# Two loads of a two-layer decode kernel, each issued as two pieces of uneven row counts

## The chip, the cores and the metric

The kernel runs on one core of one Trainium2 chip. The metric is the device time of one execution in microseconds.

## What is computed

Two layers, each an attention over a window of a cached K and V followed by a gated MLP, are applied twice in turn with the same weights to four vectors of 640 numbers, all in f32. Cut to what matters, the reference is:

```python
W = 1024                                   # the last quarter of 4096 positions
x = x + A(layernorm(x))                    # attention: 32 heads of 128, one query each
x = x + M(layernorm(x))                    # MLP: 640 -> 1728 -> 640
x = x + A(layernorm(x))
x = x + M(layernorm(x))
# A: q = x @ wq; p = softmax(q k^T / sqrt(128)) over the window; (p v) @ wo
# M: gate = x @ W_gate; h = gate * (gate > 0) * (x @ W_up); h @ W_down
```

Each number of K, V and the weights is used for only four vectors.

## The kernel before

Nearly all the work is bringing in data. The host lays K, V and the weights out as three long arrays with 128 rows, one per partition: `heads` (K, V, wq and wo of 27 heads, read in both layers), `kept` (the same of the last five heads, in the groups K0 and K1, read once and kept in the core's memory for layer two), and `mlp` (the MLP's weights). One buffer, `store`, of 128 partitions by 51,840 columns, takes all of it. A plan written at the start (`put`, `stretch`) lists which columns of which array go to which columns of `store`, in order. `load` (from L202) takes the plan's next piece whenever its place in `store` is free and issues one DMA from SP for it (L211); `done` and `free` mark columns as used up and call `load` again. SP's order is the plan's order, and the DMA queue is first in, first out on each of the 16 DMA engines. Before it reuses one of its eight landing counters, SP also waits until the load that had that counter last has landed.

Layer one (`attention(0)`) goes through nine groups of heads, K0 and K1 last. For a group TensorE computes scores (L396), VectorE and ScalarE the softmax (L403, L407), TensorE transposes the probabilities (L411) and multiplies by V (L427), then projects with wo (L461). At the end of the attention the last V product is copied out by VectorE and ScalarE (L432, L433), `free(*BACK)` gives columns back to the plan, the last projections follow, then the norm (`normalized`, L314 to L336) and the MLP (`forward`): gate and up (L519), the nonlinearity (L528, L529), a transpose (L536, L541) and W_down (L550, L561) into `y`. Layer two repeats this, with K0 and K1 first. The result is copied from `y` (L586) and stored (L587).

Two pieces of the plan matter here. The last of kept V, with the last 1,024 columns of the array up to `FRONT`, holds the last two of eight chunks of V of the last head of K1; in the plan kept W_o and wq come after it, then the first MLP weights. The last piece of all is a W_down block of 640 columns up to `MLP`, used by the last four products at L550 in layer two. Both come as 128 rows in one DMA.

Of the kernel before, what the change touches and what calls it, by code (L numbers as in the profile page):

```python
# [13 lines left out]
P = 128  # L14
# [39 lines left out]
MLP = WD1 + 3 * WD  # L54
# [7 lines left out]
FRONT = KEPT * 2 * (D + KV)  # L62
# [36 lines left out]
def decode_kernel(ctx: ExitStack, tc: tile.TileContext, x, source, sel, out):  # L99
    nc = tc.nc  # L100
# [10 lines left out]
    store = big.tile([P, STORE], F32, name="store")  # L111
# [8 lines left out]
    def put(layer, row, to, *cuts):  # L120

        for lo, hi in zip(cuts, cuts[1:]):
            assert hi - lo <= MOST and to % 64 == 0 and lo in known[row] and hi in known[row], (row, lo, hi)
            assert to + hi - lo <= STORE, (row, lo, hi, to)
            plan.append((layer, row, lo, hi, to))
            to += hi - lo
        return to

    def stretch(layer, lo, end, to):

        while lo < end:
            hi = near(min(end, lo + MOST))
            if to + hi - lo > LAP:
                to = 0
            to = put(layer, "heads", to, lo, hi)
            lo = hi
        return to
# [4 lines left out]
    def near(c, row="heads"):  # L142

        return max(x for x in ROWS[row][2] if x <= c)
# [10 lines left out]
    to = stretch(0, HELD, turn, FIRST)  # L155
# [8 lines left out]
    lo = put(0, "mlp", STORE - D, 0, D) - STORE + D  # L164
# [9 lines left out]
    to = put(1, "heads", FRONT, k, k + 1536, k + 2560, k + 3584)  # L174
# [3 lines left out]
    lo = k + 4096  # L178
    to = put(1, "heads", AHEAD[1], lo, lo + 1024, lo + 2048, lo + 3072, lo + 5120, lo + 8704)
    assert to == HOME  # L180
    lo, to = lo + 8704, HOME + BACK[1] - BACK[0]
    for n in 4608, 6144, 9728:
        hi = near(lo + n)
        to = put(1, "heads", to, lo, hi)
        lo = hi
    hi = near(lo + 4608)
    to = put(1, "heads", to, lo, hi)
    lo, hi = hi, near(hi + STORE - to)
    put(1, "heads", to, lo, hi)
    last = near(heads_end - 24704)  # L190
    to = stretch(1, hi, last, 0)
    for lo, hi in (last, near(last + 12480)), (near(last + 12480), heads_end):
        to = put(1, "heads", to if to + hi - lo <= STORE else 0, lo, hi)
    cuts = [0, 7040, 12160, GU0 + 3 * GU, WD1 + WD, MLP - 4 * D, MLP - 2 * D, MLP - D, MLP]
    for lo, hi in zip(cuts, cuts[1:]):
        to = put(1, "mlp", to if to + hi - lo <= STORE else 0, lo, hi)

    plan.reverse()

    live = [False] * STORE  # L200
# [2 lines left out]
    def load():  # L203

        if not held:
            nc.sync.dma_start(out=first_q, in_=source["heads"][:, :HELD])
        while plan and not any(live[plan[-1][4]:plan[-1][4] + plan[-1][3] - plan[-1][2]]):
            layer, row, lo, hi, to = plan.pop()
            live[to:to + hi - lo] = [True] * (hi - lo)
            held.setdefault((layer, row), []).append((lo, hi - lo, to))  # L210
            nc.sync.dma_start(out=store[:, to:to + hi - lo], in_=source[row][:, lo:hi])  # L211

    def free(a, b):
        live[a:b] = [False] * (b - a)
        load()
# [16 lines left out]
    def done(layer, row, lo, n):  # L232

        if row == "kept" and layer == 0:
            return
        if row == "kept":
            for p in range(lo, lo + n):
                if BACK[0] <= p < BACK[1]:
                    live[HOME + p - BACK[0]] = False
                elif not (AHEAD[0] <= p < AHEAD[1] or HOME <= p < HOME + BACK[1] - BACK[0]):  # L240
                    live[p] = False
        else:
            for first, m, p in held[key(layer, row)]:
                a, b = max(lo, first) - first, min(lo + n, first + m) - first
                if a < b:
                    live[p + a:p + b] = [False] * (b - a)
        load()
# [9 lines left out]

    probs = work.tile([P, W], F32, name="probs")
    load()
    gates = work.tile([P, 512], F32, name="gates")  # L260
    sel_sb = const.tile([P, P + 32], F32, name="sel_sb")
# [384 lines left out]
```

## Time and profile before

| | us |
|---|---|
| median of 3 runs (732.97 to 734.17) | 733.54 |
| the profiled execution | 733.02 |
| its span, first to last instruction | 731.2 |
| TensorE busy | 440.8 |
| VectorE busy | 76.1 |
| ScalarE busy | 50.5 |

The span is what the page's shares refer to; 1.8 us of the profiled execution lie around it. The lists further down name instructions by line, engine and operation, with the tiles written and read; what stands in brackets is the idle time of the engine before the instruction, and what ended it. The DMA share of a window is the mean busy share of the 16 DMA engines. In the list of queues, the columns are packets, megabytes, and the time of the packets as a share of 16 engines' span; q1 is SP's queue, q10 ScalarE's, and `instruction` queues bring in the program itself.

### The profile page before, as it was taken

To read this page: it belongs to the slowest core of one execution; us is meant where nothing else is said; L and a number is where in the kernel's file an instruction comes from. 1 tells how busy PE (TensorE), PEld (TensorE's weight loads), DVE (VectorE), ACT (ScalarE), POOL (GpSimd) and SP (SyncE) were. 2 spreads that over 40 slices of the span, in tenths; PEclk is the share of its full clock that TensorE was granted. 3 is DMA by queue.
4 is the path that set the end of the run, shared out by engine and by line. 5 is a ranking of instruction groups with operands and counts; after the bars stand their busy time and mean duration, and the time that the engine had idled before them with its cause. 6 is when DMAs were issued, how large, how long until landed. Compare 5 with 4: busy or idle time off the path is not lost.

```text
span 731.2 us, 8241 instructions
## 1 busy us (share of the span) xinstructions
PE 440.8 (60%) x3755; PEld 140.9 (19%) x3755; DVE 76.1 (10%) x280; ACT 50.5 (7%) x93; POOL 0.2 (0%) x4
## 2 busy tenths in 40 slices
PE   0846565655555555519778995465656556555576
PEld 0211111111111111103333231021111012111233
DVE  1111000010010101002101221001011010101011
ACT  0200000000000000000301210000000000000100
POOL 0000000000000000000000000000000000000000
PEclk9978787877777787759999999677778677877999
DMA  9999999999999999999999999999999999999996
GB/s 414 400 445 438 445 438 405 439 444 438 422 430 438 422 443 442 422 428 421 421 401 410 437 426 452 427 445 425 442 438 411 445 440 444 410 435 432 428 425 286
DMA packets 13290, 311.80 MB, mean 426 GB/s; under 512 B 1476, under 2 KB 1732, under 8 KB 6984
## 3 DMA queue, kind: packets, MB, share of 16 engines
q1 hardware_dynamic: 13104, 311.19, 99.1%
q8 instruction: 29, 0.48, 0.2%
q10 hardware_dynamic: 152, 0.09, 0.0%
q14 instruction: 5, 0.04, 0.0%
HBM read 311.19 MB, written 0.08 MB: 426 GB/s over the span
## 4 chain that ended last, share of the span: by engine, by line
DMA 75%; PE 23%; DVE 1%; issue 1%; ACT 0%; SPq 0%; ACTq 0%; DVEq 0%
DMA store<-in_heads 56%; PE ps L396 9%; DMA store<-in_kept 9%; DMA store<-in_mlp 7%; PE po L427 5%; DMA sel_sb<-in_sel 3%; PE qp L364 1%; PE pp L411 1%; PE y L461 1%; PE qp L371 1%; PE pp L396 1%; PE pp L519 1%; PE qt L383 1%; PE ot L451 0%; PE y L550 0%
## 5 line engine op out<-in xcount | busy, mean ns | idle before, releaser
L396 PE MATMUL ps<-store,qT 128*4 128x512 f32 x976 | 154.1, 711 | 119.9 <-DMA store<-in_heads 97.9
L427 PE MATMUL po<-store,pT 128*16 128x512 f32 (+1 forms) x1028 | 151.9, 708 | 122.4 <-DMA store<-in_heads 116.5
L427 PEld LDWEIGHTS po<-store,pT 128*16 128x16 f32 x1028 | 32.5, 109 | 226.9 <-issue 118.5
L396 PEld LDWEIGHTS ps<-store,qT 128*4 128x4 f32 x976 | 28.4, 95 | 227.3 <-DMA store<-in_heads 110.0
L403 DVE TENSOR_REDUCE nm<-ps 128x1 f32<-128x1024 f32 x17 | 20.8, 1225 | 255.4 <-PE ps L396 255.4
L407 ACT ACTIVATE probs<-ps,nm 128x1024 f32<-128x1024 f32 x17 | 18.9, 1113 | 328.8 <-DVE nm L403 328.8
L421 DVE COPY pT<-pp 128x16 f32<-128x16 f32 x128 | 17.1, 169 | 135.1 <-PE po L427 135.1
L461 PE MATMUL y<-store,oT 128*4 128x160 f32 x512 | 23.6, 317 | 10.6 <-DMA store<-in_heads 9.0
L438 ACT COPY gates<-po 128x512 f32<-128x512 f32 x16 | 9.4, 586 | 247.6 <-PE po L427 247.6
L519 PE MATMUL pp<-store,xT 128*32 128x256 f32 (+1 forms) x300 | 21.8, 363 | 6.7 <-DVE gates L529 3.1
L411 PE MATMUL pp<-sel_sb,probs 128*128 128x128 f32 x144 | 20.8, 293 | 0.0
L411 PEld LDWEIGHTS pp<-sel_sb,probs 128*128 128x128 f32 x144 | 18.7, 155 | 0.0
L364 PE MATMUL qp<-store,xT 128*32 128x512 f32 (+2 forms) x124 | 18.5, 586 | 0.0
L444 DVE RECIPROCAL r<-so 128x16 f32<-128x16 f32 x18 | 4.6, 257 | 131.2 <-PE so L442 131.2
L461 PEld LDWEIGHTS y<-store,oT 128*4 128x4 f32 x512 | 12.8, 90 | 19.6 <-DMA store<-in_heads 9.4
L371 PE MATMUL qp<-store,xT 128*32 128x512 f32 (+3 forms) x38 | 15.1, 505 | 0.0
L376 DVE TENSOR_SCALAR gates<-qp,rstd 128x512 f32<-128x512 f32 (+2 forms) x18 | 12.4, 690 | 17.5 <-PE qp L371 16.0
L291 PE MATMUL y<-probs,sel_sb 4*4 4x160 f32 x8 | 0.7, 444 | 21.2 <-DMA sel_sb<-in_sel 21.2
L519 PEld LDWEIGHTS pp<-store,xT 128*32 128x32 f32 x300 | 10.0, 109 | 16.3 <-DMA store<-in_mlp 7.1
L550 PE MATMUL y<-store,hT 128*4 128x160 f32 x208 | 10.3, 299 | 3.5 <-DMA store<-in_mlp 3.4
L383 PE MATMUL qt<-sel_sb,gates 128*128 128x128 f32 x64 | 12.3, 315 | 0.0
L451 PE MATMUL ot<-sel_sb,gates 128*128 128x128 f32 x72 | 11.3, 277 | 1.2 <-DVE gates L432 1.2
(79 smaller groups left out, 133.2 us busy)
## 6 DMA issues: line engine op xcount, KB each, us to landing
store<-in_heads SPq DMA_DIRECT2D x20, 7936.0 KB, 45.2
store<-in_heads SPq DMA_DIRECT2D x3, 8128.0 KB, 36.0
store<-in_mlp SPq DMA_DIRECT2D x15, 640.0 KB, 6.6
store<-in_kept SPq DMA_DIRECT2D x2, 4096.0 KB, 40.7
store<-in_heads SPq DMA_DIRECT2D x1, 8000.0 KB, 43.7
store<-in_heads SPq DMA_DIRECT2D x1, 7744.0 KB, 46.0
store<-in_heads SPq DMA_DIRECT2D x1, 7552.0 KB, 35.8
store<-in_heads SPq DMA_DIRECT2D x1, 7424.0 KB, 34.6
```

The costliest lines, as they stand in the source:

```text
L364: nc.tensor.matmul(qp[g][32 * c:32 * c + 32, a:b], xT[:, B * c:B * c + 32], part(layer, "q", g, c * n + a, b - a), start=True, stop=c > 0 ...
L371: nc.tensor.matmul(qp[g][32 * a:32 * a + 32, a * m:a * m + m], xT[:, B * c:B * c + 32], part(layer, "q", g, c * n + a * m, m), start=False ...
L376: nc.vector.tensor_scalar(gates[:, :len(HEADS[g]) * P], qp.pop(g), rstd, SCALE, op0=ALU.mult, op1=ALU.mult)
L383: nc.tensor.transpose(qt[:, i], gates[:, i * P:(i + 1) * P], ident)
L396: nc.tensor.matmul(to[32 * b:32 * b + SIDE, j, :], qT[:, at:at + SIDE], part(layer, "k", h, lo, 512), start=i == 0, stop=i == n - 1, tile_ ...
L403: nc.vector.tensor_reduce(nm[g], to.rearrange("p j n -> p (j n)"), axis=AX.X, op=ALU.max, negate=True)
L407: nc.scalar.activation(probs, sc.pop(g).rearrange("p j n -> p (j n)"), AF.Exp, bias=nm.pop(g), accum_out=sums[g])
L411: nc.tensor.transpose(pp[:, c // 4, c % 4 * P:c % 4 * P + P], probs[:, c * P:(c + 1) * P], ident)
L421: nc.vector.tensor_copy(to[:, 4 * j:4 * j + 4], pp[:, j].rearrange("p (c x) -> p c x", c=4)[:, :, i:P:32])
L427: nc.tensor.matmul(po[32 * a:32 * a + SIDE * B, x:z], t[:, at:at + SIDE * B], part(layer, "v", h, c * 512 + x, z - x), start=i == 0 and c ...
L461: nc.tensor.matmul(y[32 * a:32 * a + B], o[:, i], part(layer, "o", h, a * QUARTER, QUARTER), start=False, stop=last and h == HEADS[g][-1], ...
L519: nc.tensor.matmul(gus[j][32 * g:32 * g + 32, :2 * n], xT[:, B * c:B * c + 32], get(layer, "mlp", lo, 2 * n), start=c == 0, stop=c == KC - ...
```

## The change

```diff
+    split = {(0, "kept", FRONT): 68, (1, "mlp", MLP): 92}
     plan.reverse()
 ...
             layer, row, lo, hi, to = plan.pop()
             live[to:to + hi - lo] = [True] * (hi - lo)
             held.setdefault((layer, row), []).append((lo, hi - lo, to))
-            nc.sync.dma_start(out=store[:, to:to + hi - lo], in_=source[row][:, lo:hi])
+            rows = split.get((layer, row, hi), P)
+            for p, z in (0, rows), (rows, P):
+                if p < z:
+                    nc.sync.dma_start(out=store[p:z, to:to + hi - lo], in_=source[row][p:z, lo:hi])
```

Two loads of the plan are issued as two DMAs each: the last V block of layer one's kept part as rows 0 to 67 and rows 68 to 127, and the last W_down block of layer two as rows 0 to 91 and rows 92 to 127. The bytes, their places and the order of all other loads stay. Lines after the change are four further down.

On SP, around the kept V block, before (a row is one DMA, with rows x columns and the counters that it waits for: DMAHW0 to DMAHW7 are the eight landing counters):

```order
L211 DMA store<-in_kept 128x3072 [waits PE_49]
L211 DMA store<-in_kept 128x1024 [waits PE_49]
L211 DMA store<-in_kept 128x1920
L211 DMA store<-in_kept 128x1280 [waits DMAHW4_49]
L211 DMA store<-in_mlp 128x640 [waits DMAHW5_49,PE_49]
L211 DMA store<-in_mlp 128x1280 [waits DMAHW6_49]
L211 DMA store<-in_mlp 128x1280 [waits DMAHW7_49]
L211 DMA store<-in_mlp 128x1280 [waits DMAHW0_49]
L211 DMA store<-in_mlp 128x1280 [waits DMAHW1_49,PE_49,Activation_49]
```

The same place after the change:

```order
L215 DMA store<-in_kept 128x3072 [waits PE_49]
L215 DMA store<-in_kept 68x1024 [waits PE_49]
L215 DMA store<-in_kept 60x1024
L215 DMA store<-in_kept 128x1920 [waits DMAHW4_49]
L215 DMA store<-in_kept 128x1280 [waits DMAHW5_49]
L215 DMA store<-in_mlp 128x640 [waits DMAHW6_49,PE_49]
L215 DMA store<-in_mlp 128x1280 [waits DMAHW7_49]
L215 DMA store<-in_mlp 128x1280 [waits DMAHW0_49]
L215 DMA store<-in_mlp 128x1280 [waits DMAHW1_49]
L215 DMA store<-in_mlp 128x1280 [waits DMAHW2_49,PE_49,Activation_49]
```

The piece of 60 rows takes the counter that the next load had, and every load from there on waits for a landing one further down the list.

On SP at the end of the program, before:

```order
L211 DMA store<-in_mlp 128x2560 [waits PE_49]
L211 DMA store<-in_mlp 128x1280 [waits PE_49]
L211 DMA store<-in_mlp 128x640 [waits PE_49]
L211 DMA store<-in_mlp 128x640 [waits DMAHW3_49,PE_49]
L587 DMA out_x<-probs 128x160 [waits DMAHW4_49,DVE_49,Activation_49]
```

And after:

```order
L215 DMA store<-in_mlp 128x2560 [waits PE_49]
L215 DMA store<-in_mlp 128x1280 [waits PE_49]
L215 DMA store<-in_mlp 128x640 [waits PE_49]
L215 DMA store<-in_mlp 92x640 [waits DMAHW4_49,PE_49]
L215 DMA store<-in_mlp 36x640 [waits DMAHW5_49]
L591 DMA out_x<-probs 128x160 [waits DMAHW6_49,DVE_49,Activation_49]
```

The last piece waits for one more landing before it is issued. On TensorE the order is the same; the first product that reads the split block at L427, and the one at L550, wait for two counters in place of one.

## The prediction

> **What bounds the kernel now.** I read the page first: the span, the DMA queues, and the chain that ended last.
>
> ```profile
> span 731.2 us, 8241 instructions
> q1 hardware_dynamic: 13104, 311.19, 99.1%
> q8 instruction: 29, 0.48, 0.2%
> q10 hardware_dynamic: 152, 0.09, 0.0%
> DMA 75%; PE 23%; DVE 1%; issue 1%; ACT 0%; SPq 0%; ACTq 0%; DVEq 0%
> ```
>
> The 16 DMA engines are busy 99.1% of the span with the loads that SP issues, and 75% of the chain is DMA. The kernel is one stream of 311 MB; compute matters only where it lets the queue run dry, or at the very end. So I read the end next, the timeline of the last microseconds and the windows of half a microsecond over the same stretch (in a window: length, busy times, clock, share of the 16 engines at work, GB/s).
>
> ```profile
> 726.92 0.11 PEld L550 LDWEIGHTS y<-store,hT 128*4 128x4 f32 x8 [0.29 <-DMA store<-in_mlp]
> 727.70 0.11 PEld L550 LDWEIGHTS y<-store,hT 128*4 128x4 f32 x8 [0.67 <-DMA store<-in_mlp]
> 727.70 0.46 PE L550 MATMUL y<-store,hT 128*4 128x160 f32 x8 [0.32 <-DMA store<-in_mlp]
> 728.22 0.32 DVE L586 COPY probs<-y 128x160 f32<-128x160 f32 x1 [4.12 <-PE y L550]
> ...
> 723.50:724.00 0.50, 0.39 (x5) 0.14 (x1) 0.07 (x1) 0.00 (x0) 0.00 (x0) 1.00 0.80 328
> 724.50:725.00 0.50, 0.35 (x12) 0.30 (x16) 0.00 (x0) 0.00 (x0) 0.00 (x0) 1.00 0.61 246
> 725.50:726.00 0.50, 0.42 (x14) 0.07 (x4) 0.00 (x0) 0.00 (x0) 0.00 (x0) 1.00 0.44 174
> 726.50:727.00 0.50, 0.50 (x20) 0.19 (x12) 0.00 (x0) 0.00 (x0) 0.00 (x0) 1.00 0.32 123
> 727.00:727.50 0.50, 0.38 (x8) 0.03 (x8) 0.00 (x0) 0.00 (x0) 0.00 (x0) 1.00 0.15 56
> ```
>
> TensorE waits for the last load until 727.70 and everything after it is fixed. But the engines do not end together: the share falls from 0.80 to 0.61, 0.44, 0.32 and 0.15, so the first are out of work at about 723.9, about seven of 16 work at 725.5, five until nearly 727, and the last lands just before 727.70: a spread of 3.8 us. Each load waits for its slowest engine. The 29 instruction packets, 0.48 MB on the same engines, are the plainest cause that the page offers: an engine that fetches falls behind and, in a full stream, stays there.
>
> While few engines work each keeps its pace: 123 GB/s over 0.32 of 16 is 24 GB/s, and in full streams (below) 415 over 16 is 25.9. So nothing that all 16 share sets the pace. It is either the engine itself, or the place in the memory that it writes, which before I take to be the same eight partitions in every load of 128 rows. No row separates the two, and the change hangs on that.
>
> **Which engines the pieces use.** The loads' counts tell how rows are dealt out.
>
> ```profile
> L211 SPq DMA_DIRECT2D store<-in_heads x45: 327/328/538, 1.2 to 658.0; - x45
> L211 SPq DMA_DIRECT2D store<-in_mlp x34: 327/328/785, 347.0 to 697.0; - x34
> L211 SPq DMA_DIRECT2D store<-in_kept x10: 327/328/432, 220.9 to 341.5; - x10
> ```
>
> With the first load and the store these are 91 transfers of 128 rows, and 13104 over 91 is 144: 128 rows and 16 closings, one an engine. ScalarE's queue, 152 packets, had one such transfer (144) and x with four rows: four rows and four closings, so four engines. The largest divisor up to 16 fits both; read so, 68 rows take four engines (17 each), 60 take 15 (4 each), 92 take four (23 each), 36 take twelve (3 each). The other end, an even deal over all 16 whatever the count, would make the change worth nothing.
>
> [...]
>
> **What a row costs.** A 2,560-byte row: the last two loads of 128x640 released TensorE at 726.92 and 727.70, 0.78 us for eight rows an engine, 0.098 us each. A 4,096-byte row: 25.9 GB/s from the row below, 0.158 us.
>
> ```profile
> 357.00:359.00 2.00, 0.26 (x8) 0.07 (x8) 0.00 (x0) 0.45 (x2) 0.00 (x0) 1.00 1.00 415
> 360.00:368.00 8.00, 6.43 (x114) 3.64 (x108) 1.65 (x6) 1.47 (x5) 0.00 (x0) 1.00 1.01 417
> 371.00:373.00 2.00, 1.97 (x20) 0.56 (x18) 0.00 (x0) 0.00 (x0) 0.00 (x0) 1.00 0.96 316
> 358.96 2.17 PE L427 MATMUL po<-store,pT 128*16 128x512 f32 x16 [1.74 <-DMA store<-in_kept]
> 360.09 0.12 PEld L427 LDWEIGHTS po<-store,pT 128*16 128x16 f32 x4 [0.16 <-DMA store<-in_kept]
> store<-in_kept SPq DMA_DIRECT2D x1, 512.0 KB, 19.5
> store<-in_mlp SPq DMA_DIRECT2D x4, 640.0 KB, 6.3
> store<-in_mlp SPq DMA_DIRECT2D x3, 256.0 KB, 5.8
> DMA to landing us min/median/max: 5.1/21.3/62.4
> ```
>
> **The change, part by part.**
>
> *Two more issues on SP, and every later wait on a landing moved one load down.* An issue takes 0.33 us of an SP that mostly waits. The split V block is issued 19.5 us before it lands and the last W_down block 30 us before (the chain below), so both pieces are queued in time. The order rows show that a later load waits for the landing of one further down, for instance the W loads behind the V block; they land 18.1 us after issue, so a load's landing later (about 5 us at most, SP's longest wait for kept loads) stays covered. I cost all of it at nothing; without that cover it would be those microseconds. TensorE's last V products (L427) and last W_down products (L550) now wait for two landings in place of one: behind the first stand the projection, the norm and the gates, behind the second only a copy and the store.
>
> ```profile
> store<-in_mlp SPq DMA_DIRECT2D x3, 640.0 KB, 18.1
> SPq L211 <- DMA store<-in_kept: 10.3, 3, 4.5
> 696.96 30.70 DMA store<-in_mlp
> ```
>
> *The V block.* Four engines get 17+4 = 21 rows in place of eight, 13 x 0.158 = 2.05 us more; eleven get four, 0.63 less; one gets none, 1.26 less. *The last W_down block.* Four get 26 in place of eight, 18 x 0.098 = 1.76 more; eight get three, 0.49 less; four none, 0.78 less.
>
> *If the place sets the pace* (my forecast): the four engines now write rows of other engines' partitions, while those write too, and each has half. The V block's 17 rows take up to 5.4 us, with the other four 6.0, against 1.26: 4.7 more. They start from a lead that I estimate at 2.5 us (3.8 at the end, with 11 of the 29 instruction packets behind it at 357), so the block lands 2.2 later; bounds 0 (lead 3.8, mild sharing) and 4.7 (no lead).
>
> ```profile
> q8 instruction: 11, 0.18, 0.2%
> ```
>
> TensorE reached that block 0.16 us before it landed, so the last V product, the projection, the norm and the first gate go later by as much, and with them the loads issued as buffers come free. There the stream is thin: these land 5.8 to 6.3 us after issue where 5.1 is the shortest of the run, and at 371 to 373 the rate is already 316 of 417 GB/s. About 1 us of lateness is covered, 1.2 becomes idle engines and stays to the end. At the end the early ones of the four start the block at about 723.1; 23 rows at half pace and three more take 4.8 us, to 727.9, and one that is 1.2 us later goes to 729.1 against 727.66: +0.2 to +1.4, I take +0.6. What the late engines are relieved of does not help here, since the same partitions still take the same bytes. Sum: 1.2 + 0.6 = +1.8 us.
>
> [...]
>
> **The rivals.**
>
> *The engine sets the pace* (faster). Then it matters only who is late. At the end the five that work until 727 cannot all be among the four that get nothing, so the latest is relieved by 0.49; the four must stay under that: if they are early they end by 725.5 + 1.76 = 727.26 at worst. Gain 0.45. At the V block the late eleven are 0.63 earlier; part of that is kept, since late engines are not those that idle at 371 to 373 (between 0 and 0.63; I take 0.4). Sum -0.85. For it: each engine's pace does not depend on how many work. Against it: it needs the four to be early ones too; the decision point is 3.8 - 1.76 = 2.0 us of lead.
>
> *The four are late ones* at their own pace: the end is 1.76 later and the V block 2.05 less 1 of cover: +2.8.
>
> *It does not do what it says*: the rows are dealt evenly, or gains and losses cancel: 0, give or take 0.3.
>
> *All four write the same partitions at a time* (rows dealt in turn): five share one place, 23 rows x 0.098 x 5 = 11 us, some +8.
>
> **How the numbers follow.** The profiled execution took 733.02 (span 731.2 and 1.8 around it); the median of the runs shown is 733.54, 0.52 more, and I put the forecast beside the median. Forecast: 733.02 + 1.8 = 734.8, so 735.3 (alone 734.2 to 737.0), chance 0.47: no row favours the place over the engine, but the first rival needs a second condition and this does not. Engine: 732.2, so 732.7, 0.32. Nothing: 733.5, 0.11. Four late: 736.3, 0.06. All in one place: 741.5, 0.04. The range, 732.2 to 737.4, leaves out the lower part of the engine case and the last one. A measurement of this kernel can tell about 0.2%, 1.5 us. Slower by more: most of the forecast (0.40) and the last two (0.10), 0.50. Within: the rest of the forecast, nearly all of the engine case and the third, 0.46. Faster by more: 0.04.
>
> **What would show it.** In the windows of the end the share stays flat and drops late if the four engines are last, and falls in steps that end before 727.6 if the engine case holds. In the timeline TensorE's wait for the last kept V load ends near 362 in place of 360.09 by the forecast, and at 360 by the rival. At 371 to 373 the rate falls below 316 by the forecast. The first place that breaks it: packets of both pieces at normal pace with TensorE's V product unmoved; then sharing does not exist.

## The result, and the profile after

The changed kernel took 738.33 us (median of 4 runs, 737.61 to 740.37) against 733.27 for the kernel before beside it (4 runs): a ratio of 1.0071 with a 95% interval of 1.0049 to 1.0094, 5.1 us slower. The profiled execution took 737.61 (before 733.02). The forecast was +1.8, with 737.4 as the upper end of the range.

The page of the changed kernel, span and SP's queue:

```profile
span 735.8 us, 8245 instructions
q1 hardware_dynamic: 13107, 311.19, 99.0%
```

The same bytes in three packets more. Two whole loads have 32 closings; four pieces on 4, 15, 4 and 12 engines have 35. So the closings are those of the dealing that the prediction read; the count gives their sum, not each piece's.

Next the windows about the V block, first of the changed kernel, then those rows of the kernel before that the prediction did not show. The last three columns are TensorE's clock, the share of the 16 DMA engines and GB/s.

```profile
355.00:361.00 6.00, 1.91 (x16) 0.42 (x16) 0.00 (x0) 1.96 (x3) 0.00 (x0) 1.00 1.04 273
357.00:359.00 2.00, 0.19 (x4) 0.00 (x0) 0.00 (x0) 0.00 (x0) 0.00 (x0) 1.00 1.02 239
359.00:361.00 2.00, 0.00 (x0) 0.00 (x0) 0.00 (x0) 0.00 (x0) 0.00 (x0) 1.00 1.04 224
361.00:363.00 2.00, 1.63 (x8) 0.36 (x11) 0.00 (x0) 0.00 (x0) 0.00 (x0) 0.58 0.95 301
363.00:365.00 2.00, 1.93 (x12) 0.22 (x6) 0.00 (x0) 0.00 (x0) 0.00 (x0) 0.56 0.99 411
371.00:373.00 2.00, 1.41 (x29) 1.03 (x23) 0.44 (x2) 0.57 (x2) 0.00 (x0) 1.00 0.94 362
373.00:376.00 3.00, 3.00 (x44) 1.27 (x36) 0.00 (x0) 0.09 (x1) 0.00 (x0) 1.00 1.00 348
385.00:410.00 25.00, 22.06 (x269) 8.76 (x271) 2.87 (x10) 4.12 (x9) 0.00 (x0) 1.00 1.02 399
```

```profile
355.00:361.00 6.00, 3.95 (x32) 0.93 (x32) 0.37 (x5) 2.45 (x4) 0.00 (x0) 1.00 0.99 414
361.00:363.00 2.00, 1.40 (x22) 0.83 (x24) 0.79 (x3) 0.75 (x2) 0.00 (x0) 1.00 1.03 420
385.00:410.00 25.00, 23.03 (x268) 9.45 (x268) 5.21 (x14) 5.33 (x11) 0.00 (x0) 1.00 1.03 416
```

Read the last two columns together. From 357 to 361 the share is 1.02 and 1.04, so all 16 engines have work all the time, and yet they move 239 and 224 GB/s. Not four engines but the whole stream goes at a little over half pace. From 355 to 363 that is (414 - 273) x 6 + (420 - 301) x 2 = 1,084 KB less than before, 2.6 us at 415 GB/s.

The traces also hold the time of every single packet, and a row of a load is one packet. The V block's 128 rows of 4,096 bytes took 159 ns each before; after the change half of them took 272 ns or more. So the pieces did not go at normal pace, the first sign by which the prediction would have been broken.

TensorE at the same place in the changed kernel, then the marker where layer two's first queries begin, after and before:

```profile
361.37 3.56 PE L431 MATMUL po<-store,pT 128*16 128x512 f32 x16 [4.18 <-DMA store<-in_kept]
362.99 0.23 PEld L431 LDWEIGHTS po<-store,pT 128*16 128x16 f32 x6 [0.64 <-DMA store<-in_kept]
365.07 0.42 DVE L436 COPY gates<-po 128x256 f32<-128x256 f32 x1 [10.19 <-PE po L431]
...
402.36 0.52 PE L368 MATMUL qp<-probs,xT 128*32 128x384 f32 x2
```

```profile
361.25 0.42 DVE L432 COPY gates<-po 128x256 f32<-128x256 f32 x1 [5.88 <-PE po L427]
...
398.31 0.52 PE L364 MATMUL qp<-probs,xT 128*32 128x384 f32 x2
```

(Lines behind the edit moved down by four.) The wait for the load *ahead* of the V block, which the change does not touch, ends at 361.37 in place of 358.96; the V block's own at 362.99 in place of 360.09; the copy behind the V products comes 3.8 later, layer two's queries 4.05 later. The end of the changed kernel:

```profile
727.00:728.00 1.00, 0.79 (x17) 0.29 (x9) 0.17 (x1) 0.00 (x0) 0.00 (x0) 1.00 0.74 279
728.00:729.00 1.00, 0.07 (x4) 0.07 (x8) 0.00 (x0) 0.00 (x0) 0.00 (x0) 1.00 0.83 260
729.00:730.00 1.00, 1.00 (x32) 0.68 (x32) 0.00 (x0) 0.00 (x0) 0.00 (x0) 1.00 0.69 187
730.00:731.00 1.00, 0.20 (x8) 0.00 (x0) 0.00 (x0) 0.00 (x0) 0.00 (x0) 1.00 0.42 133
732.92 0.33 DVE L590 COPY probs<-y 128x160 f32<-128x160 f32 x1 [4.92 <-PE y L554]
```

The last copy comes at 732.92 in place of 728.22, 4.70 later: 4.05 were there at layer two's start, so 0.65 was added behind it. The stream is some 4 us later here, and from 728 to 730 the share is 0.83 and 0.69 where 4 us earlier it was 0.61 and 0.44 before; then it drops. That is nearer to the forecast's sign (flat, and late) than to the rival's. The engines still at work are slower, too: 260 GB/s over 0.83 of 16 is 20 GB/s each, 187 over 0.69 is 17, where before 246 over 0.61 was 25 and 174 over 0.44 was 25.

### The profile page after: what moved, and what is told of

Same layout as the page of the kernel before. It is cut to its first block, busy times and chain, and to the rows that moved or that the text cites. A ratio compares the mean times of both kernels' runs of the same rounds, so it can differ in the third digit from the quotient of the medians.

```text
span 735.8 us, 8245 instructions
## 1 busy us (share of the span) xinstructions
PE 440.5 (60%) x3755; PEld 140.5 (19%) x3755; DVE 76.0 (10%) x280; ACT 50.5 (7%) x93; POOL 0.2 (0%) x4
## 4 chain that ended last, share of the span: by engine, by line
DMA 73%; PE 23%; another core or an unknown queue 1%; DVE 1%; issue 1%; ACT 0%; SPq 0%; ACTq 0%; DVEq 0%
DMA store<-in_heads 53%; PE ps L400 10%; DMA store<-in_kept 9%; DMA store<-in_mlp 8%; PE po L431 6%; DMA sel_sb<-in_sel 3%; PE qp L368 1%; PE y L465 1%; PE pp L415 1%; PE qp L375 1%; PE pp L400 1%; PE pp L523 1%; PE qt L387 1%; PE ot L455 0%
## 5 line engine op out<-in xcount | busy, mean ns | idle before, releaser
L431 PE MATMUL po<-store,pT 128*16 128x512 f32 (+1 forms) x1028 | 155.1, 722 | 127.6 <-DMA store<-in_heads 118.7
L400 PE MATMUL ps<-store,qT 128*4 128x512 f32 x976 | 150.9, 698 | 118.3 <-DMA store<-in_heads 95.8
```

Of the source, the lines that this page charges most:

```text
L400: nc.tensor.matmul(to[32 * b:32 * b + SIDE, j, :], qT[:, at:at + SIDE], part(layer, "k", h, lo, 512), start=i == 0, stop=i == n - 1, tile_ ...
L431: nc.tensor.matmul(po[32 * a:32 * a + SIDE * B, x:z], t[:, at:at + SIDE * B], part(layer, "v", h, c * 512 + x, z - x), start=i == 0 and c ...
```

## The experiments

Two theories stood against each other from the prediction: **the place** (engines that write rows of each other's places in the memory share its pace) and **the engine** (each engine keeps its pace, and only the number of its rows counts).

**One part at a time.** Only the V block split, and only the W_down block:

```diff
-    split = {(0, "kept", FRONT): 68, (1, "mlp", MLP): 92}
+    split = {(0, "kept", FRONT): 68}
```

> Only the V block is split (68 and 60 rows), the last W_down block stays whole. If places shared by several DMA engines set the pace: the loss of the changed kernel in the middle, +4.1 us as its trace shows it at 401 us, stays, so +3.5 to +4.6 over before, and the rate at 355 to 361 us falls to about 273 GB/s again. If only the uneven number of rows makes four engines late, at their own pace: 0 to +1, and the rate stays above 400. If the extra issue and the moved landing counters cost it: about half of the changed kernel's +5, +2 to +3, with the rate unchanged.

```diff
-    split = {(0, "kept", FRONT): 68, (1, "mlp", MLP): 92}
+    split = {(1, "mlp", MLP): 92}
```

> Only the last W_down block is split (92 and 36 rows), the V block stays whole. Places: +0.2 to +1.2 over before (the changed kernel's trace leaves about +0.4 for the end). Uneven numbers at own pace: -0.5, since the late engines are relieved of five to eight rows. Issue and counters: +2 to +3.

V alone: 737.14 us against 733.27, ratio 1.0049 (1.0037 to 1.0061), +3.9. W_down alone: 734.17, ratio 1.001 (1.0001 to 1.0018), +0.9. The sum, 4.8, is about the 5.1 of both, so the two parts hardly touch each other and four fifths of the loss is the V block. With V alone the rate from 355 to 361 is 256 GB/s (273 with both). In the traces V alone is 4.27 late at layer two's first queries and 4.08 at the last copy, so nothing is added behind the V block's loss; W_down alone adds 0.87 behind that marker.

**Equal shares.** Both loads as rows 0 to 63 and 64 to 127: every engine gets four rows of each piece, as a mean (the 13,136 packets are 16 closings a piece), eight in all as in a whole load, so by the engine theory nothing can change.

```diff
-    split = {(0, "kept", FRONT): 68, (1, "mlp", MLP): 92}
+    split = {(0, "kept", FRONT): 64, (1, "mlp", MLP): 64}
```

> Both loads are split as rows 0 to 63 and 64 to 127, so every engine should have four and four rows, eight as before, but half of the places are in use at a time. Places: each half at half pace, 1.3 us more for the V block and up to 0.8 for the W_down block, +1.0 to +2.5 over before. Uneven numbers: 0, since no engine has more rows than before. Issue and counters: the same +5 as the changed kernel.

737.65, ratio 1.0056 (1.0044 to 1.0068), +4.4. Uneven numbers are not needed for the loss; the engine theory falls. The place theory has the sign, but its 1.0 to 2.5 is too small. The same window as above, of the halves:

```profile
355.00:361.00 6.00, 1.91 (x16) 0.42 (x16) 0.00 (x0) 2.03 (x3) 0.00 (x0) 1.00 1.02 278
```

**The same issues without the rows.** Both loads as two pieces of 128 rows and half the columns: two issues, two landing counters and double waits as in the change.

```diff
-            for p, z in (0, rows), (rows, P):
-                if p < z:
-                    nc.sync.dma_start(out=store[p:z, to:to + hi - lo], in_=source[row][p:z, lo:hi])
+            n = (hi - lo) // 2 if (layer, row, hi) in split else hi - lo
+            for c in range(0, hi - lo, n):
+                nc.sync.dma_start(out=store[:, to + c:to + c + n], in_=source[row][:, lo + c:lo + c + n])
```

> The same two loads come as two DMAs each, but split by columns: 128 rows by 512 and 512, and by 320 and 320. Issues, landing counters and double waits are those of the changed kernel, and every engine writes its own rows. Places and uneven numbers: 0, within 0.7. Issue and counters: +5.

733.43, ratio 1.0002 (0.9993 to 1.0011), and 410 GB/s from 355 to 361. The prediction's "nothing" for issues, counters and waits holds.

**Even and odd partitions.** Again two pieces of 64 rows each with four rows an engine, but interleaved:

```diff
-            for p, z in (0, rows), (rows, P):
-                if p < z:
-                    nc.sync.dma_start(out=store[p:z, to:to + hi - lo], in_=source[row][p:z, lo:hi])
+            n = 2 if (layer, row, hi) in split else 1
+            for p in range(n):
+                nc.sync.dma_start(out=store[p:P:n, to:to + hi - lo], in_=source[row][p:P:n, lo:hi])
```

> The same two loads, each split in two pieces of 64 rows, but as the even and the odd partitions in place of the lower and the upper half. Issues, landings, rows an engine and bytes are those of the halves (737.65); what differs is that an engine's four rows of a piece stay within the eight partitions that it writes in a whole load. Theory 'the place': nothing is shared by two engines, so 733.3 to 733.8, and near 410 GB/s and a full clock between 355 and 361. Rival 'a piece of fewer rows is slow in itself' (more transfers, other rows of the source, an engine that goes from piece to piece): as the halves, 736.5 to 738.

733.40, ratio 1.0 (0.9992 to 1.0009): the whole loss of the halves is gone. The same window of the even and odd pieces, 413 GB/s where the halves had 278:

```profile
355.00:361.00 6.00, 3.80 (x32) 0.95 (x32) 0.00 (x1) 2.08 (x3) 0.00 (x0) 1.00 1.00 413
```

There are as many pieces, rows, bytes, closings (13,136 packets in both) and waits; only which partitions a piece covers differs. All 128 rows of the V block take 159 ns here, as when the load is whole; half of those of the halves take 254 ns or more. So it is shown that the partitions of a piece decide.

**The price by itself.** A kernel that only loads, 24 loads of 1,024 columns (or six of 4,096) to a stage.

```diff
+    for s, (wide, pieces) in enumerate(stages):
+        for i in range(0, n, wide):
+            lo, w = (s * n + i) % 240 * cols, wide * cols
+            for rows in pieces:
+                nc.sync.dma_start(out=store[rows, i * cols:i * cols + w], in_=source["heads"][rows, lo:lo + w])
+        nc.vector.tensor_copy(probs[:, s * n % 96:s * n % 96 + n], store[:, 0:n * cols:cols])
```

> Only loads, no layers (the layers' arithmetic is left out): eleven stages of 24 loads of 1,024 columns (4,096-byte rows), each stage ended by one VectorE copy that waits for all of them; in the last four stages six loads of 4,096 columns. Rows of each stage: all 128 whole; halves 64 and 64; 68 and 60; 92 and 36; even and odd; 0 to 63 alone; the even ones alone; 0 to 31 alone; every fourth alone; 0 to 3 alone; 0, 32, 64 and 96 alone. Theory 'the place': each group of eight partitions takes about 26 GB/s whoever writes it. Whole, even and odd, even alone, every fourth: 410 to 420 GB/s; halves between 210 and 300, 0 to 63 alone 210, 0 to 31 alone 105, 0 to 3 alone 26, and the four rows in four places 105. 68 and 60, 92 and 36: between the halves and the whole. Rival 'the engine': halves, 64 alone and 32 alone 415, 0 to 3 alone 105 as the four rows far apart; 68 and 60 bound by four engines with 21 rows of 128, some 158 GB/s; 92 and 36 by four with 26, some 128.

This kernel, like the two load kernels behind it, ran once. Windows inside ten of the eleven stages, in that order (whole; halves; 68 and 60; 92 and 36; even and odd; 0 to 63 alone; even alone; 0 to 31 alone; 0 to 3 alone; 0, 32, 64 and 96 alone). Behind the window's length stand VectorE, GpSimd, TensorE's clock, the share of the engines and GB/s:

```profile
30.00:58.00 28.00, 0.00 (x0) 0.00 (x0) 1.00 1.03 412
65.00:110.00 45.00, 0.00 (x0) 0.00 (x0) 1.00 1.04 241
120.00:200.00 80.00, 0.00 (x0) 0.00 (x0) 1.00 0.43 143
210.00:305.00 95.00, 0.00 (x0) 0.00 (x0) 1.00 0.33 124
315.00:343.00 28.00, 0.00 (x0) 0.00 (x0) 1.00 1.01 388
350.00:376.00 26.00, 0.00 (x0) 0.00 (x0) 1.00 1.04 208
382.00:396.00 14.00, 0.00 (x0) 0.00 (x0) 1.00 0.97 360
402.00:416.00 14.00, 0.00 (x0) 0.00 (x0) 1.00 0.94 192
433.00:443.00 10.00, 0.00 (x0) 0.00 (x0) 1.00 0.25 26
448.00:453.00 5.00, 0.00 (x0) 0.00 (x0) 1.00 0.25 56
```

Rows 0 to 63 keep all engines at work (share 1.04) and reach 208, half of the 412 of whole loads; 64 rows that are spread (even alone) reach 360. Several expectations missed. Rows 0 to 31 reach 192, not 105, so a place is not eight partitions in a row: 0 to 31 reach as many places as 0 to 63. Rows 68 and 60 and 92 and 36, repeated, give 143 and 124 at a share of 0.43 and 0.33: that fits four engines with most of the rows as the bound, for which the engine theory had 158 and 128. Four rows far apart gave 56, not 105, though four rows in one place gave 26. That is two places at the 26 GB/s of one, two rows in each; which rows share one, this stage does not tell. The packets fit it too: a row of 16,384 bytes takes 0.61 us on every fourth partition, 1.17 us with these four rows and 2.40 us with rows 0 to 3, as with one, two and four rows in a place at a time. Pieces that are spread fell short by less: 388 for even and odd, 360 and 358 for the even ones and every fourth alone, where 410 to 420 were expected. The prediction does not say which eight partitions make a place; the expectation above counted eight in a row.

**One cut among whole loads.** In that kernel only load 13 of 24 is cut:

```diff
+            for rows in one if i == 12 else most:
+                nc.sync.dma_start(out=rows(store[:, i * cols:(i + 1) * cols]), in_=rows(source["heads"][:, lo:lo + cols]))
```

> Only loads again (the layers' arithmetic is left out): twelve stages of 24 loads of 1,024 columns, each ended by a VectorE copy that waits for all. In the first nine only load 13 of 24 is cut: not at all; 64 and 64; 68 and 60; 92 and 36; even and odd; three pieces 32 to 95, 0 to 31, 96 to 127; then, behind a load of 12,288 columns on every fourth of rows 0 to 31 (eight rows, to make some engines late), not at all; 64 and 64; 68 and 60. The last three: rows 32 to 95 alone, 0 to 15 alone, whole again. Theory 'the place, lower and upper half apart': rows 0 to 63 and 0 to 31 both reached about 200 GB/s in the stages before, so a place is not eight partitions in a row, and half of all places lie below partition 64 and half above. Then 32 to 95 alone reaches 340 or more (0 to 63: 208), one load in halves costs 1.3 us, 68 and 60 about 2 to 2.7 (four engines with 13 rows of 0.159 us more, and sharing), 92 and 36 about 2.9 to 3.5 (18 rows), even and odd 0 to 0.3, three pieces under 1. Where engines are late the halves cost 1.3 to 2.6. Theory 'eight partitions in a row are a place': 32 to 95 alone 208, three pieces as the halves. Rival 'sharing costs more than its bytes': halves 2.5 or more in even step.

The copies that end the stages (a stage lasts from one copy's start to the next one's): whole to 59.68; then halves, 68 and 60, 92 and 36, even and odd, three pieces; to 366.30 rows 32 to 95 alone, and to 416.53 the second whole stage. For these last two the idle time in brackets and the copy before it (0.18) make the stage.

```profile
59.68 0.18 DVE L131 COPY probs<-store 128x24 f32<-128x24 f32 x1 [20.43 <-DMA store<-in_heads]
94.57 0.18 DVE L131 COPY probs<-store 128x24 f32<-128x24 f32 x1 [34.70 <-DMA store<-in_heads]
132.65 0.18 DVE L131 COPY probs<-store 128x24 f32<-128x24 f32 x1 [37.90 <-DMA store<-in_heads]
171.96 0.18 DVE L131 COPY probs<-store 128x24 f32<-128x24 f32 x1 [39.13 <-DMA store<-in_heads]
205.44 0.18 DVE L131 COPY probs<-store 128x24 f32<-128x24 f32 x1 [33.30 <-DMA store<-in_heads]
...
366.30 0.18 DVE L131 COPY probs<-store 128x24 f32<-128x24 f32 x1 [19.88 <-DMA store<-in_heads]
416.53 0.18 DVE L131 COPY probs<-store 128x24 f32<-128x24 f32 x1 [33.32 <-DMA store<-in_heads]
```

The first three cuts end at 94.57, 132.65 and 171.96. The whole stage lasts 33.50. Halves cost 34.89 - 33.50 = 1.39, as expected; 68 and 60 cost 4.58, 92 and 36 5.81, both far over what was expected here. The 4.58 is close to the prediction's upper bound for the V block, 4.7, in which all rows of the big piece go at half pace. Even and odd cost nothing (205.44 - 171.96 = 33.48), the three pieces 0.69. Rows 32 to 95 alone take 20.06 us, where 0 to 63 alone took 32.8 and the even ones alone 20.13: that fits if the lower and the upper 64 partitions are the two halves of the places. The 56 of the four rows far apart then fits if rows 0 and 32 share one place and rows 64 and 96 another. Rows 0 to 15 alone take 16.73 us, half of 32.8 for a quarter of the rows, as with half as many places. The stages with a late load tested nothing: that load ran beside the end of the stage before (that whole stage took 33.47, no longer than without it).

**Engines out of step.** So one or two loads of eight rows were put inside the stage, to make half of the engines late:

```diff
+            for k in range(late if i == 4 else 0):
+                nc.sync.dma_start(out=aside[0:32:4, 12288 * k:12288 * (k + 1)], in_=source["heads"][0:32:4, 12288 * k:12288 * (k + 1)])
```

> Only loads (the layers' arithmetic is left out): ten stages of 24 loads of 1,024 columns, each ended by a VectorE copy that waits for all. Between load 4 and load 5 come none, one or two loads of 12,288 columns for every fourth of rows 0 to 31, eight rows, which make half of the engines late by about 1.9 us each (49,152 bytes at 26 GB/s). Load 13 is whole, cut in halves, in even and odd, or in 68 and 60. Stages: whole; one late load with whole, halves, even and odd; two late loads with whole, halves, even and odd; halves without a late load; two late loads with 68 and 60; whole. A cut's price is its stage less the whole one with as many late loads. Theory 'engines out of step pay more': in the kernel, whose engines are up to 3.8 us apart, halves cost 4.4 for two loads where 1.39 and, by bytes, 0.87 are the price in step; so 2.0 to 2.8 here with one or two late loads, 1.4 without. Rival 'the price is the bytes': 1.4 in each, and what is more in the kernel comes behind the load, where the stream is thin. Even and odd: 0 to 0.3 by both. 68 and 60 with two late loads: 4.6 as in step by the rival.

The copies of the stages: whole, then with one late load whole, halves, even and odd, then with two late loads whole and halves, and halves without a late load between 284.71 and 319.69.

```profile
59.74 0.18 DVE L129 COPY probs<-store 128x24 f32<-128x24 f32 x1 [7.69 <-DMA store<-in_heads]
94.87 0.18 DVE L129 COPY probs<-store 128x24 f32<-128x24 f32 x1 [25.32 <-DMA store<-in_heads]
134.00 0.18 DVE L129 COPY probs<-store 128x24 f32<-128x24 f32 x1 [29.36 <-DMA store<-in_heads]
169.52 0.19 DVE L129 COPY probs<-store 128x24 f32<-128x24 f32 x1 [25.68 <-DMA store<-in_heads]
206.30 0.18 DVE L129 COPY probs<-store 128x24 f32<-128x24 f32 x1 [25.45 <-DMA store<-in_heads]
247.45 0.18 DVE L129 COPY probs<-store 128x24 f32<-128x24 f32 x1 [29.12 <-DMA store<-in_heads]
```

With one late load the whole stage takes 35.13 (33.33 without: 1.8 late, about the 1.9 us of one row of 49,152 bytes at 26 GB/s, so the eight rows are taken to lie on eight engines, one each; no run counts them by engine) and the halves 39.13: the cut costs 4.00, with two late loads 41.15 - 36.78 = 4.37, without 34.98 - 33.33 = 1.65. Even and odd cost 0.4 and 0.5, 68 and 60 with two late loads 5.0. So with engines out of step the halves cost 2.4 to 2.6 times the price, more than the 2.0 to 2.8 us expected; the rival, 1.4 in each, falls. For 68 and 60, the cut of the change, being out of step matters little: 5.0 in place of 4.58. That the halves cost 4.4 in the kernel, whose engines are up to 3.8 us apart, where 1.39 and, by bytes, 0.87 are the price in step, fits this, but the two loads were not priced apart there. The packets show where the time goes: 202 rows of the stage with halves and no late load take over 200 ns, 319 with one late load and 387 with two, 34 to 43 in whole stages. The cut load has only 128 rows, so rows of whole loads about it are slowed as well. Which engines they meet is argued only: an engine that is ahead writes into places whose own engines are still busy with earlier loads, and both lose.

**What carries it to the end: TensorE or the stream?** After its long wait TensorE got a clock of 0.58, and its V products took 3.56 us. Products of the identity with itself fill the wait:

```diff
+            if last and layer == 0 and i == n - 1:
+                for _ in range(18):
+                    nc.tensor.matmul(pp[:, 0, :P], ident, ident, start=True, stop=True)
```

> The changed kernel, plus 18 products of the identity with itself (128x128, about 0.2 us each by the rows of such products, some 3.8 us) in layer one while TensorE waits for the load ahead of the split V block. It loads nothing more and leaves nothing out. The last V products should then take near 2.2 us at a granted clock near 1.0, in place of 3.56 at 0.58 and 0.56. Theory 'the clock carries part of it': TensorE is what is late after the block, so about 1.3 us of the 5 come back, 737.0 with 0.5 either way. Rival 'the stream has lost it already': while the pieces are written the engines move 224 to 273 GB/s in place of 415, those bytes are not made up, and TensorE's slower products lie beside that; then 738.3 as the changed kernel, with 0.4 either way.

The window behind the filled wait, and the products:

```profile
361.00:363.00 2.00, 2.00 (x16) 0.54 (x14) 0.00 (x0) 0.00 (x0) 0.00 (x0) 1.00 0.93 319
361.33 2.99 PE L434 MATMUL po<-store,pT 128*16 128x512 f32 x16
```

The clock stays at 1.00 and the products end earlier (364.3 in place of 364.9), yet the time is 737.96 (737.2 to 739.52), ratio 1.0059 (1.0045 to 1.0073): within the changed kernel's interval, and 1.0 above the 737.0 of the clock theory. So the clock is not what carries the loss to the end.

And the other way round: the two loads of the change whole, and a load of the same size split for which TensorE does not wait.

```diff
-    split = {(0, "kept", FRONT): 68, (1, "mlp", MLP): 92}
+    split = {(1, "heads", k + 4096 + 2048): 68}
```

> The kernel before, with neither load of the change split, but a load of the same size (128x1024, the second one behind the K cache of layer two's first group) as rows 0 to 67 and 68 to 127; TensorE does not wait for it where it lands, at about 406. Theory 'the stream sets the end': the engines lose the same while they share, whoever waits, and nothing later gives it back: 735 to 736.5, 1.7 to 3 above the kernel before. Rival 'only the wait costs': nobody waits at that place, so 733.3 to 734, and the loss of the change came from TensorE's wait and what stands behind it.

735.69, ratio 1.0034 (1.0021 to 1.0046), +2.4, as the stream theory said. Windows of that kernel, and the longest of TensorE's waits between 395 and 425:

```profile
400.00:405.00 5.00, 4.97 (x59) 1.87 (x55) 1.22 (x3) 0.96 (x2) 0.00 (x0) 1.00 0.99 342
405.00:410.00 5.00, 4.42 (x37) 1.15 (x26) 1.91 (x3) 2.49 (x4) 0.00 (x0) 1.00 1.04 233
410.00:415.00 5.00, 5.00 (x45) 1.98 (x44) 0.68 (x3) 0.00 (x0) 0.00 (x0) 1.00 1.02 374
PE po L431 <- DVE pT L425: 1.0, 1, 1.0
```

TensorE's longest wait is 1.0 us and for VectorE, so 233 GB/s passes it unnoticed; the time is lost all the same. Against 410, 440 and 441 GB/s before, the three windows lack 1,710 KB, 4.0 us at 430 GB/s, and this profiled execution took 737.15, 4.1 above the one before. Some of that is not the split's: layer two's first queries, ahead of it, already came 0.92 later (399.23). The median, +2.4, is the fairer price.

## Why the prediction was wrong

- **What bounds the kernel**: right, and the reason for the loss: a stream that fills 99% of the span gave nearly nothing back (V alone: 4.27 late at layer two's first queries, 4.08 at the last copy).
- **The dealing out of rows**: right (three packets more; an even deal of four pieces over 16 engines would have been 32 more). That the four engines of a big piece also get rows of the small one, 21 and 26 in all, no run shows by itself: the closings have no engine's number. The repeated pieces of the load kernel are near it, 143 and 124 GB/s, where by estimate, at the trace's 0.159 us a row, 21 and 26 rows on the busiest engine make 157 and 127, 17 and 23 alone make 194 and 143. **Issues, counters, waits at nothing**: right (columns, 1.0002).
- **The place or the engine**: the right choice; the halves and the even and odd pieces decide it. That rows which share a place go at half pace was its assumption; measured, half of the block's rows took 272 ns or more in place of 159, and rows 0 to 63 alone ran at 208 GB/s where whole loads had 412. What it left open is which partitions make a place: they are not eight in a row (rows 0 to 31 alone had 192 GB/s, not 105). Rows 64 to 127 were not run alone. The prediction counted only the time of the four engines with most rows; in the trace the whole stream slowed down (239 and 224 GB/s at a share of 1.02 and 1.04).
- **The step that failed**: the V block's term, 1.2. It was 4.7 for rows at half pace, less a lead of 2.5 ("the block lands 2.2 later"), less a cover ("About 1 us of lateness is covered, 1.2 becomes idle engines"). The 4.7 was about right: 4.58 in the load kernel. The two deductions are what failed: the term measured 3.9 (V alone), so they were worth 0.8 together in place of 3.5. The block's landing came out near (2.9 later), but it is not the price: the sharing slowed all 16 engines, the load ahead of the block came later too (2.4 at its wait), and 2.6 us of bytes were gone by 363. A cover at TensorE does not give these back: split where TensorE does not wait, a load of this size still costs 2.4.
- **The lead**: the 2.5 was an estimate, and its own count, 11 of 29 instruction packets behind 3.8 us, would give 1.4. No run shows that these packets put the engines apart, or that the four are early ones. Engines that are out of step did not make the cut cheaper in the load kernel: 5.0 in place of 4.58 for 68 and 60, 4.0 in place of 1.65 for halves.
- **The end**: +0.6 forecast; +0.65 in the trace behind layer two's start, +0.9 with W_down alone. Right, and the slower engines at the end fit its reason.
- **The sign at 371 to 373**: wrong. The rate there is 362, above 316; TensorE comes later, and a thin stretch lies behind (348 from 373 to 376, 411 before).
- **The rivals**: "the engine sets the pace" would have given a gain; that halves with equal shares lose 4.4 excludes it. "The four are late ones" (+2.8) needs engines at their own pace and falls with it. "It does not do what it says" falls with the three packets and the loss. "All four write the same partitions" had some 8 us for the W_down block, which alone cost 0.9.

**Still open**: between 363 and layer two's start the lateness grows by some 1.4 us more (2.6 us of bytes by 363, 4.05 at the marker; 399 GB/s in place of 416 from 385 to 410). It was not tried apart, and traces without a split V block have this marker 0.2 to 1.25 later than the one before (398.49 with columns, 399.56 with W_down alone), so how much of it belongs to the change is not known. What a cut costs from one place to another (2.4 and 3.9 for the same load size) was not traced to single engines either. And in every run a row of the source goes to the partition of the same number. That the shared place lies in the core's memory, and not at the source, is therefore argued; no run parts the two.

## What to carry to other kernels

Where a stream of loads sets the time, price a load by what it does to the rate of all engines, not by when it lands: look for windows in which the share stays at 1 and the GB/s fall (here 1.04 and 224, where 415 was the rate before). Cut a load by columns, or interleave its partitions (neither cost anything here for two cut loads, ratios 1.0002 and 1.0, though even and odd pieces one after another moved 388 GB/s in place of 412), but do not cut it into a lower and an upper part of the partitions (+4.4 us for two loads in halves). And do not count on a lead or on cover to pay for a conflict of places: with engines out of step one load in halves cost 4.0 to 4.4 us, in step 1.4 to 1.65.

## What the runs showed of the hardware that was not expected

- Rows 0 to 63 alone ran at 208 GB/s, 0 to 31 alone at 192, 32 to 95 alone in 20.06 us where 0 to 63 took 32.8, the even partitions alone at 360, rows 0, 32, 64 and 96 alone at 56 where rows 0 to 3 had 26.
- One load in halves among whole ones cost 1.4 to 1.65 us with the engines in step and 4.0 to 4.4 behind one or two late loads of eight rows, which made the whole stage 1.8 or 3.5 us longer.
- After a wait of 4.2 us TensorE's granted clock was 0.58 and 0.56 for some 4 us; 18 small products in the wait kept it at 1.00.
